# The order and the queue of the first loads of a four-layer kernel

## The chip, the cores and the metric

The kernel runs on one core of a Trainium2 chip. The metric is the device time of one execution in microseconds (us). Every run quoted here is fast, with a granted TensorE clock of 0.999 or 1.000 over the whole run. A profile gives the span of one execution; where a run was profiled, its time as a run is 1.7 to 2.0 us longer than its span. That offset is taken as it is. In lines of the profile PE is TensorE (PEld its weight loads), DVE is VectorE, ACT is ScalarE and SP is SyncE; a q behind the name is the engine's queue of instructions, and L404 is line 404 of the kernel.

## The reference

Four layers on x of 2048 rows by 1024 columns in bf16: layer norm, then linear attention (A), layer norm, then a gated feed-forward (B), and both again with the same weights.

```python
def _layernorm(x, axis=-1, eps=1e-5):
    m = jnp.mean(x, axis=axis, keepdims=True)
    v = jnp.var(x, axis=axis, keepdims=True)
    return (x - m) / jnp.sqrt(v + eps)
...
x = A_x
x = x + _A_ref(_layernorm(x, axis=-1), A_wqkv, A_wo)
x = x + _B_ref(_layernorm(x, axis=-1), B_W_gate, B_W_up, B_W_down)
x = x + _A_ref(_layernorm(x, axis=-1), A_wqkv, A_wo)
x = x + _B_ref(_layernorm(x, axis=-1), B_W_gate, B_W_up, B_W_down)
```

Only the first 20 us matter here: the first four blocks of 128 rows of x are normed, turned over by TensorE and multiplied with the first two column halves (512 columns each) of the key weights, called k0 and k1. q0 is the first half of the query weights.

## The kernel before

The head of the program warms TensorE with ten idle matmuls and issues the first loads, the blocks of x on ScalarE's queue and the weights on SyncE's:

```python
for _ in range(10):
    nc.tensor.matmul(idle, lhsT=zero[:, 0:P], rhs=zero, start=True, stop=True)

k0, k1, v0, q0, q1 = (ring.place() for _ in range(5))
self.load_x(0, 0, nc.scalar)
self.load_x(0, 1)
self.load_x(1, None, nc.scalar)
k0(0, H)
self.load_x(2, None, nc.scalar)
k0(H, 2 * H)
self.load_x(3, None, nc.scalar)
k1()
q0()
self.load_x(4)
...
```

`load_x(t, c)` loads half c of block t, or all of it. `k0(0, H)` loads the first four of k0's eight slices of 128 rows. The sizes are 256 KB for a block of x, 512 KB for half of k0 and 1024 KB for k1 or q0.

What follows is in program order on VectorE and ScalarE, with the work of block 1 woven into that of block 0:

```python
def block0():
    stat(0, 0)
    stat(0, 1)
    rstd(0)
    stat(1, 0)        # block 1's load is waited for here
    scale(0, 0)       # ... ahead of the scale of block 0
    scale(0, 1)
    t0 = turn(0, 0)
    t1 = turn(0, 1)
    t0("s")
    stat(1, 1)
    rstd(1)
    t1("v")
    k(0, 0, between)  # 8 matmuls with k0; turns half of block 1 before the last 2
...
def block1():
    turn(1, 1)("v")
    norm(2)           # block 2's load is waited for here
    k(1, 0)
...
return [block0, block1, lambda: k(0, 1), lambda: block(1, 1, 2), lambda: k(2, 0),
        lambda: block(2, 1, 3), lambda: k(3, 0), lambda: k(3, 1)]
```

## Time and profile before

| | before |
|---|---|
| median of the first 3 runs | 1629.3 us (1629.21 to 1630.51) |
| the profiled run, as a run and as a span | 1630.68 and 1628.9 us |
| TensorE busy | 1621.7 us |
| first projection matmul | 7.46 us |
| fifth projection matmul, after the wait for k0 | 10.23 us |
| VectorE begins the statistics of block 2 | 12.08 us |
| transposes of block 3 | 19.28 us |

TensorE is busy all the time but for the head, so the table is a list of the moments in the head that set the rest. The last row serves as a clock in this document: the span is that moment plus, here, 1628.9 - 19.28 = 1609.6.

### The profile page before, as it was taken

How to read it: one execution, taken by the hardware profiler on the slowest of the kernel's cores; microseconds unless marked ns; L12 is line 12 of the kernel's file. 1: busy time of each engine (PE TensorE's matmuls, PEld its weight loads, DVE VectorE, ACT ScalarE, POOL GpSimd, SP SyncE). 2: the span in 40 equal slices, each digit the busy share in tenths (PEclk: the TensorE clock that was granted, in tenths of full speed). 3: DMA queues.
4: the chain of work that ended last, by engine and by line, in shares of the span. 5: the costliest groups of instructions: out<-in, count | busy, mean ns of one | idle time of the engine just before them, and what ended most of it. 6: DMA issues, size and time to landing. Idle time of an engine off the chain costs nothing.

```text
span 1628.9 us, 18772 instructions
## 1 busy us (share of the span) xinstructions
PE 1621.7 (100%) x7754; PEld 739.3 (45%) x7754; DVE 566.7 (35%) x940; ACT 331.8 (20%) x638; POOL 201.9 (12%) x134
## 2 busy tenths in 40 slices
PE   8999999999999999999999999999999999999999
PEld 4444444444444444444444444444444444444444
DVE  7845695213212222212165547942022111111211
ACT  5741212101110110111066312121011101101110
POOL 2349220000000000000023592100000000000000
DMA  7312647448445444544560147464554454454452
GB/s 245 65 52 56 178 71 206 144 148 232 155 143 190 160 151 161 168 147 137 168 128 1 53 93 250 85 193 146 182 165 152 155 184 155 145 166 154 155 162 71
DMA packets 298246, 235.06 MB, mean 144 GB/s; under 512 B 101296, under 2 KB 294192, under 8 KB 298160
## 3 DMA queue, kind: packets, MB, share of 16 engines
q1 hardware_dynamic: 292832, 228.75, 47.7%
q10 hardware_dynamic: 5328, 5.11, 0.9%
q8 instruction: 60, 0.98, 0.3%
q14 instruction: 26, 0.21, 0.0%
HBM read 201.33 MB, written 8.39 MB: 129 GB/s over the span
## 4 chain that ended last, share of the span: by engine, by line
PE 98%; ACT 1%; DVE 1%; DMA 1%; issue 0%; SPq 0%; DVEq 0%
PE pu L639 24%; PE pg L639 24%; PE acc L663 23%; PE ps L404 12%; PE ps L530 7%; PE ps L439 7%; DMA t<-in_A_wqkv_dram 1%; PE kv L452 0%; PE acc_last L663 0%; ACT e L351 0%; ACT e L350 0%; PE fold L515 0%; DVE st L138 0%; ACT e L352 0%; DVE slab L358 0%
## 5 line engine op out<-in xcount | busy, mean ns | idle before, releaser
L639 PEld LDWEIGHTS <-t 128*128 128x128 bf16 x3584 | 350.3, 98 | 423.2
L639 PE MATMUL pu<-xnT,t 128*128 128x512 bf16 x1792 | 423.5, 379 | 0.0
L639 PE MATMUL pg<-xnT,t 128*128 128x512 bf16 x1792 | 423.4, 379 | 0.0
L663 PE MATMUL acc<-t,hT 128*128 128x512 bf16 x1764 | 382.5, 379 | 0.0
L645 DVE TENSOR_TENSOR hT<-pu,rg 128x512 bf16<-128x512 f32 x224 | 154.7, 691 | 572.0 <-PE pu L639 572.0
L644 ACT ACTIVATE rg<-pg 128x512 f32<-128x512 f32 x224 | 133.5, 596 | 737.3 <-PE pg L639 737.0
L663 PEld LDWEIGHTS <-hT 128*128 128x128 bf16 x1820 | 177.9, 98 | 209.1
L404 PE MATMUL ps<-t,xnT 128*128 128x512 bf16 x1024 | 224.3, 380 | 2.2 <-DMA t<-in_A_wqkv_dram 1.7
L404 PEld LDWEIGHTS <-xnT 128*128 128x128 bf16 x1024 | 99.2, 98 | 122.3 <-issue 4.3
L530 PE MATMUL ps<-T,pqT 128*128 128x512 bf16 x512 | 111.2, 379 | 0.0
L145 ACT ACTIVATE rstd<-mv,eps 128x1 f32<-128x1 f32 x64 | 18.7, 293 | 334.1 <-DVE mv L143 333.9
L680 DVE TENSOR_TENSOR xo<-x,acc 128x512 bf16<-128x512 f32 x31 | 21.3, 688 | 170.3 <-PE acc L663 170.3
L483 POOL TENSOR_TENSOR prod<-pq,zrow 128x1024 f32<-128x1024 bf16 x32 | 67.9, 2122 | 85.9 <-DVE den L488 72.5
L138 DVE BATCH_NORM_STATS2 stats<-x 128x6 f32<-128x512 f32 (+1 forms) x120 | 78.0, 673 | 0.8
L530 PEld LDWEIGHTS <-pqT 128*128 128x128 bf16 x512 | 49.9, 98 | 60.4 <-issue 0.5
L419 POOL CAST ksum<-x 128x512 f32<-128x512 bf16 x2 | 1.7, 866 | 605.4 <-DVE x L358 605.4
L677 DVE TENSOR_TENSOR x<-x,acc 128x512 f32<-128x512 f32 x32 | 21.6, 675 | 138.5 <-PE acc L663 137.4
L421 POOL TENSOR_TENSOR ksum<-ksum,slab 128x512 f32<-128x512 f32 x46 | 54.0, 1183 | 84.6 <-DVE slab L358 75.1
L358 DVE SCALAR_TENSOR_TENSOR pq<-ps,e 128x512 bf16<-128x512 f32 x64 | 44.0, 688 | 53.9 <-ACT e L352 52.2
L495 POOL TENSOR_TENSOR pq<-pq,den 128x1024 bf16<-128x1024 bf16 x32 | 61.7, 1933 | 3.1 <-DVE den L490 3.1
L488 DVE TENSOR_REDUCE den<-prod 128x32 f32<-128x1024 f32 x32 | 39.0, 1217 | 53.9 <-POOL prod L483 53.9
L439 PE MATMUL ps<-slab,x 128*128 128x512 bf16 x256 | 56.6, 379 | 0.0
(57 smaller groups left out, 596.0 us busy)
## 6 DMA issues: line engine op xcount, KB each, us to landing
t<-in_B_W_gate_dram SPq DMA_DIRECT2D x56, 1024.0 KB, 7.1
t<-in_B_W_up_dram SPq DMA_DIRECT2D x56, 1024.0 KB, 5.4
t<-in_B_W_down_dram SPq DMA_DIRECT2D x64, 896.0 KB, 5.2
t<-in_A_wqkv_dram SPq DMA_DIRECT2D x11, 1024.0 KB, 5.6
t<-in_A_wo_dram SPq DMA_DIRECT2D x4, 1024.0 KB, 7.2
away<-x SPq DMA_DIRECT2D x8, 512.0 KB, 4.4
x<-away SPq DMA_DIRECT2D x8, 512.0 KB, 8.5
out_dram<-xo ACTq DMA_DIRECT2D x31, 128.0 KB, 2.5
```

The lines of the kernel that those rows point to most:

```text
L138: self.nc.vector.bn_stats(out=stats[:, c, :], in_=src[:, c * fmax:(c + 1) * fmax])
L358: nc.vector.scalar_tensor_tensor(out=out, in0=ps, scalar=0.0, in1=e, op0=ALU.max, op1=ALU.add)
L404: nc.tensor.matmul(by_row(ps), lhsT=self.xnT[l, l_q][:, kt, j * P:(j + 1) * P], rhs=w[:, kt, :].rearrange("p (b i d) -> p i b d", i=R, d=H ...
L421: nc.gpsimd.tensor_tensor(out=ksum[:, cols], in0=ksum[:, cols], in1=pk, op=ALU.add)
L439: nc.tensor.matmul(ps, lhsT=self.xn[l, t][:, d * P:(d + 1) * P], rhs=self.pk[l, t][:, h * NW:(h + 1) * NW], start=(t == 0), stop=(t == sel ...
L483: nc.gpsimd.tensor_tensor(out=prod, in0=pq_of[sc, j], in1=zrow, op=ALU.mult)
L495: nc.gpsimd.tensor_tensor(out=heads(pq), in0=heads(pq), in1=den[:, :].unsqueeze(2).to_broadcast([P, D // HD, HD]), op=ALU.mult)
L530: nc.tensor.matmul(ps, lhsT=pqT[sc][:, g, j * P:(j + 1) * P], rhs=T[g // 2][:, g % 2, n2 * NW:(n2 + 1) * NW], start=(g == 0), stop=(g == G ...
L639: nc.tensor.matmul(ps, lhsT=w[:, kt, fi * P:(fi + 1) * P], rhs=self.xnT[l, q][:, kt, :], start=(kt == 0), stop=(kt == KT - 1))
L644: nc.scalar.activation(out=rg, in_=pg, func=ACT.Relu)
L645: nc.vector.tensor_tensor(out=h[:, fi, :], in0=pu, in1=rg, op=ALU.mult)
L663: nc.tensor.matmul(ps[:, 0:n], lhsT=hT[ft // 4][:, ft % 4, j * P:(j + 1) * P], rhs=wd[:, k, i * n:(i + 1) * n], start=(ft == 0), stop=(ft ...
```

## The change

The change puts the first loads all on SyncE's queue, in an order meant to bring k0 sooner: block 0, half of k0, block 1, the other half of k0, k1, and only then blocks 2 and 3. The aim is that the second half of k0, for which TensorE waits 1.7 us, no longer shares the way with blocks 2 and 3 (512 KB).

```diff
-        self.load_x(0, 0, nc.scalar)
+        self.load_x(0, 0)
         self.load_x(0, 1)
-        self.load_x(1, None, nc.scalar)
         k0(0, H)
-        self.load_x(2, None, nc.scalar)
+        self.load_x(1)
         k0(H, 2 * H)
-        self.load_x(3, None, nc.scalar)
         k1()
+        self.load_x(2)
+        self.load_x(3)
         q0()
```

## The prediction

> **What bounds the kernel now.** I read the page first, then the waits of TensorE, then the first 30 us as a timeline, as the chain of work and as DMA landings. On the page TensorE is busy 1621.7 of 1628.9 us. The waits view of TensorE over the whole span has four rows, all in the head of the kernel:
> ```profile
> PE ps L404 <- DMA t<-in_A_wqkv_dram: 1.7, 1, 1.7
> PE idle L220 <- DVE zero L217: 1.3, 1, 1.3
> PE tp L260 <- DVE x L154: 0.6, 1, 0.6
> PE ps L404 <- ACT xnT L267: 0.4, 1, 0.4
> ```
> Columns: total us, times, longest. The same view from 20 us on is empty. So all that loads can still give lies before 20 us, and only one row, 1.7 us, names a load: the second half of the first weights (k0). The timeline of the head shows where:
> ```profile
> 0.74 0.40 SPq L369 DMA_DIRECT2D x<-in_A_x_dram  x1
> 0.76 1.97 ACTq L369 DMA_DIRECT2D x<-in_A_x_dram  x4
> 1.19 3.78 SPq L35 DMA_DIRECT2D t<-in_A_wqkv_dram  x4
> 3.78 1.29 DVE L138 BATCH_NORM_STATS2 st<-x 128x6 f32<-128x512 bf16 x2 [2.49 <-DMA x<-in_A_x_dram]
> 5.22 0.68 DVE L138 BATCH_NORM_STATS2 st<-x 128x6 f32<-128x512 bf16 x1
> 5.90 0.74 DVE L154 TENSOR_SCALAR x<-x,mv,rstd 128x512 bf16<-128x512 bf16 x2
> 7.46 1.04 PE L404 MATMUL ps<-t,xnT 128*128 128x512 bf16 x4 [0.37 <-ACT xnT L267]
> 10.23 0.59 PE L404 MATMUL ps<-t,xnT 128*128 128x512 bf16 x2 [1.73 <-DMA t<-in_A_wqkv_dram]
> 12.08 1.28 DVE L138 BATCH_NORM_STATS2 st<-x 128x6 f32<-128x512 bf16 x2
> ```
> Columns: start, length. VectorE takes block 0 at 3.78, the first statistic of block 1 at 5.22, scales block 0 at 5.90; TensorE runs four matmuls of the first projection and stops at 8.50, until k0's second half is there. The last row is the statistics of the third block. The chain of work between 8 and 20 us says what the end depends on after that:
> ```profile
> 1.66 8.53 DMA t<-in_A_wqkv_dram
> 10.19 0.04 issue
> 10.23 0.59 PE ps L404 x2
> ...
> 11.74 0.42 DVE xnT L265
> 12.16 1.20 DVE st L138 x2
> ...
> 18.72 0.51 DVE x L154
> 19.23 0.05 issue
> 19.28 0.62 PE tp L260 x8
> ```
> All but the first lines of it is **VectorE**: from the copy at 11.74 to the scale at 18.72 it works in program order with hardly a gap (busy 0.86 to 1.00 in each microsecond from 12 to 19), and TensorE's 0.6 us wait at 19.28 is for it. From there on the chain never leaves busy engines. So a gain in the head is worth what it moves **VectorE's work at 12.08**, no more.
>
> **What the Trainium skill says.** "DMA: Bandwidth & Descriptors", section "Issuing engines are not separate DMA queues": loads issued from several engines run on the same 16 DMA engines and interleave; several issuers save only issue time. The trace agrees: 388 GB/s at 4 to 5 us with both queues, 350 at 12 to 13 us with SyncE's alone, so one queue loses little bandwidth and the change is one of order. Section "Queues, rings and completion order": each DMA engine takes turns between queues, and completion is not in order of issue. The trace agrees: x block 2, on ScalarE's queue, was issued after half of k0 was, and landed at 7.5, well before it (10.2). Section "Why a DMA increments its semaphore by 16 and not by 1": the 16 engines finish independently and only the full count means landed. In the view of DMA packets in 0.2 us steps the packets under 512 B (with these loads I take them for the completion writes) of k1 come from 10.6 to 13.0 us, so the slowest engine is over 2 us behind the others. That matters below.
>
> **The part removed: ScalarE's four issues and the turn-taking.** They take 1.97 us of ScalarE's queue (row at 0.76); ScalarE's first work on block 0 comes at 5.34, so this frees nothing on the path.
>
> **The part added: the same loads on SyncE.** An issue takes 0.40 to 0.51 us, so the eight first loads go out at about 0.74, 1.19, 1.6, 2.1, 2.6, 3.0, 3.5, 4.0. First bytes move some 1.5 us after an issue (0.74 to 2.2), and each load's turn comes later than that, so issue time is hidden.
>
> **The part moved: the order of bytes.** Landings before, from issue plus time to landing of the DMA view: block 0 at 3.55 and 3.8, block 1 at 5.2, first half of k0 at 5.7, block 2 at 7.5, second half of k0 at 10.2, block 3 at 10.4, k1 at 13.4, q0 at 16.4. I turn this into a landing rate, from 2.2 us on and including the slowest engine: up to the first half of k0, 1024 KB in 3.5 us, 293 KB/us; up to k1, 3072 KB in 11.2 us, 274; up to q0, 4096 KB in 14.2, 288. The second half of k0, 2048 KB in 8.0, had only 256, as part of k1 went beside it. With 274 to 293 KB/us, as an estimate, the new order lands so:
> - block 1: 1024 KB, 5.7 to 5.9 (was 5.2)
> - second half of k0: 1536 KB, 7.4 to 7.8, at 256 KB/us 8.2 (was 10.2)
> - k1: 2560 KB, 10.9 to 11.5 (was 13.4)
> - block 2: 2816 KB, 11.8 to 12.5 (was 7.5)
> - block 3: 3072 KB, 12.7 to 13.4 (was 10.4; used at 14.98)
>
> Now the path. (a) Block 0 comes alone first; its statistic may start up to 0.3 us sooner, and the second half, issued 0.45 us later than before, is needed only 0.6 us after the first. (b) VectorE takes block 1's statistic before it scales block 0, so it waits until about 5.75 instead of 5.22, and block 0's scale goes from 5.90 to 5.75 + 0.68 = 6.43: **0.5 us lost**. (c) The four first matmuls then run from 8.0 to 9.0, and k0's second half is there (8.2 at worst): the wait of 1.73 us is gone, the fifth matmul starts at 9.0 instead of 10.23, **1.2 us gained** on TensorE. (d) VectorE could then take block 2 at 12.08 - 1.2 = 10.9, but block 2 lands at 11.8 to 12.5. Its statistics start between 0.2 us earlier and 0.45 later than now, about **0.1 us later** in the middle. VectorE's chain and with it the end move by that, not by 1.2.
>
> **Rivals.** *The full gain.* If the lag of the slowest engine comes from two queues taking turns, it is gone: 2816 KB at 0.37 MB/us, the rate of the typical engine, is 7.8 us, with 0.5 us to the semaphore it lands at 10.5, before 10.9. Then 1.2 us are gained: 1628.1 us. For it: there is hardly any spread until 5.4 us. Against it: after 10 us SyncE's queue runs alone and the lag stays at 2 us. *A new wait takes its place*, that of block 2, as worked out: 1629.4; at the late end, or if the lag is another half microsecond larger, 1629.8 to 1630.3. *SyncE's queue as the bound*: its fourth weight load took 1.39 us to issue and the next block 4.59 us, so the queue can block when much is outstanding. But block 2 goes out after about as much as stood before that 1.39 us, so its block would be some 1 us, and its turn for the DMA engines comes at about 9.5 us: hidden. *Later loads starve*: q0 and the fifth block keep their place in the sum of bytes (q0 16.4, fifth block 17.05, used near 26.8 and 21.8): hidden.
>
> **Range and chances.** I give the new wait 65% (0.1 us slower) and the full gain or most of it 35% (1.0 us faster): 0.065 - 0.35 = -0.3 us, so 1629.3 - 0.3 = 1629.0 us. The runs before lie between 1629.2 and 1630.5, so scatter is as large as the effect; with the two rivals' ends I take 1627.8 to 1630.6. Two per cent are 32.6 us, ten times all of TensorE's waits: within 2% 0.98, 0.01 on each side.
>
> **What would show it.** TensorE's wait for k0 is gone or under 0.3 us, and its fifth matmul starts near 9.0 (c). VectorE's first statistic of block 1 waits on its load and starts at 5.6 to 6.0 (b). VectorE's statistics of block 2 have a load as releaser and start at 11.8 to 12.5 (d); if they start near 10.9 with no load named, the rival of the full gain holds. The eight transposes of block 3 (19.28 now) move by as much as that start, and the span with them. I am wrong if they move and the span doesn't, if block 2 lands much later than 12.5, or if the order of loads changes what the scheduler makes of the later engine programs, which would show as a difference after 20 us.

## The result, and the profile after

The changed kernel takes 1631.9 us in the median of 4 runs (1631.48 to 1633.01), against 1629.32 for the kernel before in the same session. The ratio is 1.0015, with a 95% interval of 0.9998 to 1.0033. Ratios here are the mean time of one kernel's fast runs over that of the other's fast runs of the same rounds, so they are not quite the ratio of the medians. At the 2% level this is "same", as forecast; but the time lies above the stated range (1627.8 to 1630.6), and all four runs lie above all runs of before. The middle of the forecast, 0.3 us faster, had the other sign, too.

The programs of TensorE, VectorE and GpSimd are instruction for instruction the same in both kernels; only the issues of loads moved. So nothing but landings, and what follows from them, can explain the difference. The waits of TensorE over the whole span of the changed kernel:

```profile
PE tp L260 <- DVE x L154: 2.9, 1, 2.9
PE idle L220 <- DVE zero L217: 1.3, 1, 1.3
PE ps L404 <- ACT xnT L267: 0.3, 1, 0.3
```

The wait of 1.7 us for k0 is gone, as intended. In its place TensorE waits 2.9 us ahead of its first transposes, for VectorE's scale of block 0. The timeline of the head says why (start, length, engine, instruction, and in brackets the idle time before it with what ended it):

```profile
2.13 0.51 SPq L369 DMA_DIRECT2D x<-in_A_x_dram  x1
...
2.98 1.28 DVE L138 BATCH_NORM_STATS2 st<-x 128x6 f32<-128x512 bf16 x2 [1.69 <-DMA x<-in_A_x_dram]
...
7.64 0.69 DVE L138 BATCH_NORM_STATS2 st<-x 128x6 f32<-128x512 bf16 x1 [3.14 <-DMA x<-in_A_x_dram]
8.25 0.72 DVE L154 TENSOR_SCALAR x<-x,mv,rstd 128x512 bf16<-128x512 bf16 x2
...
8.71 1.03 PE L260 MATMUL tp<-ident,x 128*128 128x128 bf16 x8 [2.91 <-DVE x L154]
...
10.00 2.74 PE L404 MATMUL ps<-t,xnT 128*128 128x512 bf16 x6 [0.26 <-ACT xnT L267]
...
14.43 1.27 DVE L138 BATCH_NORM_STATS2 st<-x 128x6 f32<-128x512 bf16 x2
```

The first row is the issue of block 1 at 2.13. Block 0 is used sooner than before, at 2.98 instead of 3.78. Then VectorE waits 3.14 us for block 1, which lands at 7.62 (2.13 plus the 5.49 us that the chain of work gives it); before, its statistic ran at 5.22. Block 0's scale stands behind that statistic in program order and goes from 5.90 to 8.25. The row at 10.00 holds a second surprise: six matmuls take 2.74 us, while before the first four took 1.04. The view of that line of code gives the records of single matmuls in ns (minimum, median, maximum), for the changed kernel from 11 to 12 us:

```profile
L404 PE MATMUL ps<-t,xnT x4: 634/634/634, 10.4 to 11.7; 128*128 128x512 bf16 x4
```

and for the kernel before from 7 to 8 us:

```profile
L404 PE MATMUL ps<-t,xnT x3: 380/380/390, 7.5 to 7.9; 128*128 128x512 bf16 x3
```

TensorE had stood idle from 5.80 to 8.71 and ran at half its pace, a matmul every 0.43 us instead of every 0.22, until about 13.5 us. The Trainium skill describes this on "TensorE: Matmul & The Clock Gate", section "Part 1: The HAM clock gate (the "warmup" mystery)": the array runs at half clock by default, comes up after some 3.4 us of sustained matmuls and goes back when idle. The trace agrees with its figures for 512 columns, 426.7 and 215.7 ns from start to start. The column of the granted clock in the table of windows reads 1.00 in these same microseconds. The records of clock changes that lie behind it are in the packed trace, though no view lists them: the first of this run is the rise to full clock at 13.49 us, and ahead of a first record the column reads 1.00 whatever the clock is. So, as far as the records go, the clock did not fall here: the ten idle matmuls (4.45 us, 0.43 us apart) had not brought it up. In eight of the other profiles it rose between 4.87 and 6.59 us; three traces hold no such record.

The chain of work in the changed kernel:

```profile
2.13 5.49 DMA x<-in_A_x_dram
7.62 0.02 issue
7.64 0.04 DVE st L138
...
10.00 2.74 PE ps L404 x6
12.74 0.43 PE tp L260 x4
...
14.08 0.42 DVE xnT L265
14.51 1.20 DVE st L138 x2
...
21.63 0.62 PE tp L260 x8
```

It runs through block 1's load and the slow matmuls, not through block 2's load, which the forecast had named. The transposes of block 3 come at 21.63 instead of 19.28, and 21.63 - 19.28 = 2.35 is the difference of the spans (1631.2 - 1628.9 = 2.3). For this pair of profiles the sum closes: +2.42 for block 1's statistic (5.22 to 7.64), -1.73 for the wait that is gone, and the rest, 2.35 - 2.42 + 1.73 = 1.66, is nearly all the slow clock (six matmuls at 0.21 us extra are 1.3, the transposes and the last two the rest).

It would be easy to stop here. But a pair of profiles is two executions, and the experiments show that this is only a part of the story.

### The profile page after: what moved, and what is told of

The parts are those of the page before. It is cut to its first block, busy times and chain, and to the rows that moved or that the text cites. A ratio compares the mean times of both kernels' runs of the same rounds, so it can differ in the third digit from the quotient of the medians.

```text
span 1631.2 us, 18772 instructions
## 1 busy us (share of the span) xinstructions
PE 1623.6 (100%) x7754; PEld 740.7 (45%) x7754; DVE 566.5 (35%) x940; ACT 331.6 (20%) x638; POOL 201.9 (12%) x134
## 4 chain that ended last, share of the span: by engine, by line
PE 98%; ACT 1%; DVE 1%; DMA 0%; issue 0%; SPq 0%; DVEq 0%
PE pu L639 24%; PE pg L639 24%; PE acc L663 23%; PE ps L404 12%; PE ps L530 7%; PE ps L439 7%; PE kv L452 0%; PE acc_last L663 0%; DMA x<-in_A_x_dram 0%; ACT e L351 0%; ACT e L350 0%; PE fold L515 0%; DVE st L138 0%; ACT e L352 0%; DVE slab L358 0%
```

## The experiments

The theory at the outset: the changed order costs through block 1, which is late behind half of k0, and through the slow clock that this brings with it. Rivals: block 2 behind k1 sets the pace, as forecast; the single queue itself is slow; the profiles are not typical. Twelve runs were made, of eight new kernels and four repeats, all correct. "Mean against before" is the ratio of fast runs, turned into us with 1629.6.

| run | block 1's statistic, us | block 2's statistics, us (load waited for) | block 3's transposes, us | span, us | median run, us | mean against before |
|---|---|---|---|---|---|---|
| before, first profile | 5.22 | 12.08 (no) | 19.28 | 1628.9 | 1629.3 | |
| before_again_1 | 5.24 | 11.08 (no) | 18.29 | 1627.9 | 1629.42 | 0.9997 |
| before_again_2 | 5.27 | 10.45 (no) | 17.65 | 1627.3 | 1629.04 (one run) | |
| changed, first profile | 7.64 | 14.43 (no) | 21.63 | 1631.2 | 1631.9 | 1.0015, +2.4 us |
| after_again | 6.26 | 12.68 (yes, 0.34) | 19.90 | 1629.5 | 1631.84 | 1.0015, +2.4 us |
| a_after_24_idle | 6.91 | 12.45 (no) | 19.66 | 1629.3 | 1631.49 | 1.0010, +1.6 us |
| i_after_x2_before_k1 | 6.97 | 13.51 (no) | 20.70 | 1630.3 | 1631.44 | 1.0011, +1.8 us |
| d_x1_before_k0 | 5.22 | 12.52 (yes, 1.73) | 19.73 | 1629.3 | 1631.08 | 1.0008, +1.3 us |
| f_before_no_idle | 5.64 | 11.82 (no) | 19.02 | 1628.6 | 1630.55 | 1.0006, +1.0 us |
| c_before_order_one_queue | 5.20 | 10.99 (no) | 18.48 | 1628.1 | 1630.48 | 1.0004, +0.7 us |
| b_x0_x1_on_act | 5.46 | 11.03 (yes, 0.61) | 18.24 | 1627.9 | 1630.11 | 1.0003, +0.5 us |
| h_one_queue_best | 5.94 | 12.21 (no) | 19.41 | 1629.0 | 1629.78 | 1.0002, +0.3 us |
| e_best | 5.32 | 10.20 (no) | 17.39 | 1627.0 | 1628.95 | 0.9999, -0.2 us |
| e_again | 5.25 | 10.12 (no) | 17.32 | 1626.9 | 1628.79 | 0.9994, -1.0 us |

All intervals of the ratios but that of after_again (1.0002 to 1.0027) reach over 1, as the scatter of single runs, up to 2 us, is as large as the effects. So the runs are read together with the profiles, where the mechanism shows.

### Keep TensorE busy in the changed kernel

```diff
-        for _ in range(10):
+        for _ in range(24):
```

> The changed kernel with 24 instead of 10 idle matmuls ahead of the first work, nothing else. In the changed kernel TensorE stands idle from 5.8 to 8.7 us and its first projection matmuls then start every 0.43 us instead of every 0.22. Theory 'cold clock': busy through 5.8 to 8.5, the matmuls from 10.0 us on start every 0.22 us (records of 380 ns, not 634), the copy that VectorE makes at 14.08 comes near 12.8, block 2 (landed at 12.7 in the changed kernel) lets its statistics start near 12.9 instead of 14.43, and the transposes of block 3 come at 20.0 to 20.2 instead of 21.63; span about 1629.7, that is 1.5 us below the changed kernel and still 0.8 above before. Rival 'only the late load of block 1': the matmuls stay slow or the end doesn't move; transposes of block 3 at 21.6, span 1631.2.

Measured: 24 idle matmuls ran from 1.35 to 8.72 us, the first ten at 0.43 us each and the rest at 0.22. The first six projection matmuls took 1.47 us instead of 2.74, so the clock was up (its record rises at 5.47), and the copy on VectorE that had ended the slow stretch at 14.08 came at 12.02. The span was 1629.3, near the 1629.7 expected. The edit is not clean in one respect: the idle matmuls themselves held TensorE until 8.72, while the scale of block 0 was begun at 7.52. From the first transposes to that copy it took 3.46 us instead of 5.37, so by this pair the slow clock cost 1.9 us in the first profile (1.7 by the sum above). The runs gained less than the profile: +1.6 us against before instead of +2.4. A term of the clock is there, but with it gone the kernel is still slow.

### The changed order with block 0 and block 1 back on two queues

```diff
-        self.load_x(0, 0)
+        self.load_x(0, 0, nc.scalar)
         self.load_x(0, 1)
         k0(0, H)
-        self.load_x(1)
+        self.load_x(1, None, nc.scalar)
         k0(H, 2 * H)
```

> The changed order, but the first half of block 0 and block 1 go back to ScalarE's queue; block 2 and 3 stay on SyncE behind k1. Theory 'one queue is late to start and puts block 1 behind half of k0': block 1 lands near 5.2 us again, its statistic starts at 5.2 to 5.4, TensorE stays warm, the second half of k0 lands by 8.2 (it has 512 KB less ahead of it than before) so the wait of 1.73 us is under 0.3; block 2 then limits: lands at 11.8 to 12.7, transposes of block 3 at 19.1 to 19.9, span 1628.7 to 1629.5. Rival 'the order of block 2 and 3 behind k1 alone costs it': block 1 is at 5.2 but the span stays near 1631.

Measured: block 1's statistic came at 5.46, TensorE stayed fast, and no load of k0 was waited for. Block 2 landed at 11.0, somewhat sooner than the 11.8 to 12.7 expected, and VectorE waited 0.61 us for it. The span was 1627.9 and the runs only 0.5 us over before. Most of the loss is gone, but the edit changes the queue as well as block 1's turn, and block 2 landed at 11.01 instead of 12.66 to 12.74, so this run alone doesn't say which of them did it.

### The order of before on one queue

```diff
+        self.load_x(1)
         k0(0, H)
-        self.load_x(1)
-        k0(H, 2 * H)
-        k1()
         self.load_x(2)
+        k0(H, 2 * H)
         self.load_x(3)
+        k1()
         q0()
```

> The order of the kernel before, but all on SyncE's queue: block 0, block 1, half of k0, block 2, half of k0, block 3, k1. Theory 'order': block 1 has only block 0 ahead of it and lands by 5.0 us, TensorE stays warm, the second half of k0 has 2048 KB up to it as before and lands at 9.5 to 10.3, so the end is that of before within 0.5 us: 1628.9 to 1629.4 in the profile. Rival 'the single queue itself' (issue in a row, the DMA engines stand idle between 2.8 and 3.6 us in the changed kernel): the idle of the DMA engines comes again and the span is 1630 or more.

Measured: block 1's statistic at 5.20 and the second half of k0 landed at 9.10, with a wait of 0.76 us for it and a wait of 0.48 us for k1, which landed at 12.81. The span was 1628.1, better than expected of either theory, and the runs 0.7 us over before. **The single queue costs 0.7 us in the mean here, not 2.4.** Two other pairs of runs differ in the queue: block 1 early (1.3 over before on one queue, in the run after this one, and 0.5 on two, in the run before), and the two further orders below (0.3 and -0.2). They read 0.8 and 0.5. Each is within the scatter, but all three have one sign. It does leave a mark. In the table of windows the last figures of a row are the granted clock, the DMA engines' busy share and GB/s. The kernel before from 3 to 4 us:

```profile
3.00:4.00 1.00, 1.00 (x4) 0.42 (x3) 0.22 (x1) 0.00 (x0) 0.00 (x0) 1.00 1.07 385
```

and the changed kernel:

```profile
3.00:4.00 1.00, 1.00 (x4) 0.41 (x3) 1.00 (x2) 0.00 (x0) 0.00 (x0) 1.00 0.69 174
```

With one queue the DMA engines move less than half as much for a microsecond. I read it so, without a run that shows it: the small halves of block 0 are done before the next load, issued 0.92 us after the first, has come to flow. The run with the order of before has the same hole (180 GB/s from 3 to 4 us, 230 from 4 to 5), but there the busy share is 1.13 from 3 to 4, so the engines weren't simply empty. In that run block 1's own packets (2.9 to 4.9 us) fall into the hole, and it still lands at 5.17; in the changed kernel those of half of k0 do, ahead of block 1.

### Block 1 ahead of k0, the rest as changed

```diff
+        self.load_x(1)
         k0(0, H)
-        self.load_x(1)
         k0(H, 2 * H)
```

> The changed kernel with one swap: block 1 ahead of the first half of k0, all on SyncE's queue. Theory 'order of block 1': block 1 lands by 5.0 us (was 7.62), its statistic is no longer waited for beyond that, the first projection matmul comes at 7.5 to 8.0 unless the first half of k0, then fourth in line, lands later than that (6.96 in the changed kernel, with 256 KB more ahead 7.5 to 8.0); TensorE stays warm; block 2 limits at 12.0 to 12.7, transposes of block 3 at 19.3 to 20.0, span 1629.0 to 1629.6. Rival 'the single queue': k0's first half is late too, over 8.5 us, TensorE cools, span over 1630.5.

Measured: as expected, but for block 1, which landed at 5.20 and not by 5.0. The timeline of VectorE:

```profile
5.22 0.69 DVE L138 BATCH_NORM_STATS2 st<-x 128x6 f32<-128x512 bf16 x1 [0.77 <-DMA x<-in_A_x_dram]
...
12.52 1.29 DVE L138 BATCH_NORM_STATS2 st<-x 128x6 f32<-128x512 bf16 x2 [1.73 <-DMA x<-in_A_x_dram]
```

Block 1's statistic is back at 5.22, TensorE is fast, k0 is waited for 0.32 us, and now VectorE waits 1.73 us for block 2, which lands at 12.50. The transposes of block 3 are at 19.73 and the runs 1.3 us over before. This shows the forecast's term by itself: block 2 behind k1 sets a floor of 12.5 us.

### The changed kernel once more

No edit.

> The changed kernel itself once more, on another chip session, to see how much of its profile is chance: is block 1 late again, does TensorE cool again? Theory 'block 1 behind half of k0, then the cold clock': block 1 lands at 6.7 to 7.7 us, the first projection matmuls start every 0.43 us, the transposes of block 3 come at 20.5 to 21.7, mean of the fast runs 2 to 3 us over before. Rival 'one unlucky profile': block 1 lands before 6.2 or the matmuls are fast, and the mean is within 1 us of before.

Measured: the runs repeat, +2.4 us, but the profile doesn't look like the first. The timeline of VectorE and TensorE:

```profile
6.26 0.69 DVE L138 BATCH_NORM_STATS2 st<-x 128x6 f32<-128x512 bf16 x1 [1.71 <-DMA x<-in_A_x_dram]
...
12.68 1.29 DVE L138 BATCH_NORM_STATS2 st<-x 128x6 f32<-128x512 bf16 x2 [0.34 <-DMA x<-in_A_x_dram]
```

```profile
8.62 2.38 PE L404 MATMUL ps<-t,xnT 128*128 128x512 bf16 x6 [0.26 <-ACT xnT L267]
```

Block 1 was used at 6.26 instead of 7.64, below the 6.7 expected. TensorE was still slow for most of its first six matmuls. This time the chain goes through block 2's load, landed at 12.66, and the span is 1629.5. So one and the same kernel ends now by block 1 and the clock, now by block 2. It is the fastest of its five runs that was profiled. Both expectations missed in part: the profile was better than the theory said, and the mean didn't move.

### Two further orders

With block 1 early and block 2 between k0 and k1, first on two queues:

```diff
-        self.load_x(0, 0)
+        self.load_x(0, 0, nc.scalar)
         self.load_x(0, 1)
+        self.load_x(1, None, nc.scalar)
         k0(0, H)
-        self.load_x(1)
         k0(H, 2 * H)
-        k1()
         self.load_x(2)
+        k1()
         self.load_x(3)
         q0()
```

> First half of block 0 and block 1 on ScalarE's queue, the rest on SyncE's in the order second half of block 0, both halves of k0, block 2, k1, block 3, q0. Theory: the head is a chain of three landings (block 1, second half of k0, block 2) and the clock; here block 1 lands by 5.5, k0 by 7.6, block 2 by 9.0, k1 by 11.4, so no load is waited for after block 1. VectorE takes block 2 at 10.3 to 10.5 instead of 12.08, transposes of block 3 at 17.5 to 18.0 instead of 19.28; profile's span 1627.1 to 1627.6, mean of the fast runs 1 to 1.7 us under before, faster than the run with block 2 behind k1 (1627.9 in its profile). Rival 'TensorE or VectorE has another limit there' (k1 in time, 8 matmuls of k1 at 11.7): transposes of block 3 stay at 18.2 or later.

Measured: no load is waited for after block 1, and the chain is TensorE's and VectorE's own work:

```profile
7.47 1.47 PE ps L404 x6
...
10.28 1.20 DVE st L138 x2
...
17.39 0.62 PE tp L260 x8
```

The second half of k0 lands at 7.4 and block 2 at 8.0. The span is 1627.0, a bit better than expected, but the mean is only 0.2 us under before (with one longer run, 1630.5, among five), where 1.0 to 1.7 was expected. That miss pointed at the kernel before: its first profile might not be typical.

The same order with all on SyncE's queue:

```diff
+        self.load_x(1)
         k0(0, H)
-        self.load_x(1)
         k0(H, 2 * H)
-        k1()
         self.load_x(2)
+        k1()
         self.load_x(3)
```

> As the run before it in order, but all on SyncE's queue with block 1 ahead of k0: block 0, block 1, both halves of k0, block 2, k1, block 3, q0. Theory 'order decides, the queue little': block 1 at 5.2, both halves of k0 by 8.8, block 2 by 9.8, k1 by 12.2; a wait for k0 of 0.3 and for k1 of 0.5 at most, transposes of block 3 at 18.0 to 18.6, span 1627.6 to 1628.2, 0.3 to 0.8 above the two-queue form. Rival 'the single queue itself costs the 2 us': span 1630 or more.

Measured: the runs are 0.3 us over before, as expected of order; the profiled run (1630.81) was the slowest of the five and shows how that comes about:

```profile
7.00 1.03 PE L260 MATMUL tp<-ident,x 128*128 128x128 bf16 x8 [1.22 <-DVE x L154]
8.30 2.66 PE L404 MATMUL ps<-t,xnT 128*128 128x512 bf16 x6 [0.26 <-ACT xnT L267]
```

Block 1 landed at 5.92 instead of 5.2. TensorE stood idle for 1.22 us and then ran slow for over 2 us; the first record of its clock is the rise at 10.73, so here, too, the ten idle matmuls had not brought it up. The expected 18.0 to 18.6 became 19.41. Of this delay of some 1.1 us, the slow clock alone accounts for about as much: 2.66 instead of 1.47 us for six matmuls.

### The kernel before without warming

```diff
-        for _ in range(10):
+        for _ in range(1):
```

> The kernel before with one idle matmul instead of ten; loads as before. It measures the cold clock by itself: nothing of the loads moves. Theory 'cold clock': the first projection matmuls start every 0.43 us instead of 0.22 (records of 634 ns instead of 380); 0.21 us more for each of them after the wait for k0 (10.23), some 4 to 12 until the clock is back, so the copy at 11.74 comes 0.9 to 1.5 us later and the transposes of block 3 at 20.2 to 21.0; span 1629.8 to 1631.5. Rival 'the clock is no matter here, as VectorE limits from 12 us on': transposes of block 3 within 0.3 us of 19.28.

Measured, with the loads of before:

```profile
8.00 2.56 PE L404 MATMUL ps<-t,xnT 128*128 128x512 bf16 x6 [0.26 <-ACT xnT L267]
```

The matmuls are slow, and the runs are 1.0 us over before. Block 2 was ready all along, so this is nearly a price of the clock by itself; block 1 was also 0.4 us later in this profile (5.64). The position expected for the transposes (20.2 to 21.0) was too late. It was reckoned from the first profile of before, and in this one the second half of k0 landed at 9.3 and was not waited for.

### The kernel before, profiled twice more

No edit.

> The kernel before, profiled once more. The first profile of it took 1630.7 us as a run, 1.4 over its median, so it may be an unlucky one. Theory 'the second half of k0 landed late by chance in that profile': in a typical run it lands near 9 us, the wait for it is 0.5 us or less instead of 1.7, VectorE takes block 2 at 10.6 to 11.2 instead of 12.08, the transposes of block 3 come at 17.8 to 18.4 and the span is 1627.4 to 1628.0; then the removed wait was mostly not there to win. Rival 'the first profile is typical': wait 1.5 to 1.8 us, span 1628.7 to 1629.1.

> As the run ahead of it, a second look at the kernel before: by the theory the second half of k0 lands between 8.5 and 10.2 us and the span is its start of block 3's transposes plus 1609.6 us; by the rival both looks show the 1.7 us.

Measured: the timeline of TensorE in the first of them and in the second.

```profile
9.23 0.59 PE L404 MATMUL ps<-t,xnT 128*128 128x512 bf16 x2 [0.81 <-DMA t<-in_A_wqkv_dram]
```

```profile
7.42 1.77 PE L404 MATMUL ps<-t,xnT 128*128 128x512 bf16 x6 [0.37 <-ACT xnT L267]
```

The wait for the second half of k0 is 0.81 us in one and doesn't show as a wait in the other: six matmuls run in 1.77 us, against 1.47 with no load late. The load landed at 9.19 and 8.56, against 10.19 in the first profile. VectorE takes block 2 at 11.08 and 10.45. The wait of 0.81 is more than the 0.5 that the theory allowed, but in the main it holds: **the 1.7 us that the change was to save were an unlucky execution.** The spans say the same: of the 25 of before in the three later sessions, with a median of 1627.7, only two reach the 1628.9 of the first profile. As runs these two took 1629.69 and 1629.04, on either side of the median; the first profile took 1630.68.

### Block 2 ahead of k1, block 1 left behind half of k0

```diff
-        k1()
         self.load_x(2)
         self.load_x(3)
+        k1()
         q0()
```

> The changed kernel with blocks 2 and 3 moved ahead of k1, nothing else: one queue, block 1 still behind half of k0. Theory 'two terms: block 2 behind k1 sets the floor at 12.5 to 12.7, block 1 behind half of k0, with the cold clock, is the other': block 2 lands by 10, k1 at 11.7 to 12.7, block 1 still at 6.3 to 7.6, TensorE cold; VectorE takes block 2 at 11.9 to 14.4 as TensorE lets it, the runs lie 0.3 to 1.0 us under the changed kernel and still 1 to 2 over before. Rival 'block 2 is all of it': within 0.5 us of before. Rival 'block 1 is all of it': as the changed kernel, 2.0 to 2.5 over before.

Measured: block 2 landed at 9.1 and was not waited for. Block 1 still landed at 6.95, and then:

```profile
8.04 0.72 PE L260 MATMUL tp<-ident,x 128*128 128x128 bf16 x8 [2.24 <-DVE x L154]
...
9.12 2.74 PE L404 MATMUL ps<-t,xnT 128*128 128x512 bf16 x6 [0.37 <-ACT xnT L267]
```

Here the column of the granted clock does show it, with 0.50:

```profile
10.00:11.00 1.00, 1.00 (x4) 0.40 (x3) 0.48 (x2) 0.00 (x0) 0.00 (x0) 0.50 1.08 376
```

By its records the clock rose at 5.70, fell at 9.11 and rose again at 12.52. So the transposes at 8.04 ran at full pace (0.72 us for eight, against 1.03 in the changed kernel) and the matmuls at 9.12 did not.

The runs are 1.8 us over before and the transposes of block 3 at 20.70. Taking away the late block 2 alone (this run) leaves 1.8 of the 2.4 us; taking away the late block 1 alone (block 1 ahead of k0) leaves 1.3; taking away both on one queue leaves 0.3. So each of the two lateness terms is enough to lose more than a microsecond: one repair alone takes away 0.6 or 1.1 of the 2.4 us, both together 2.1. What lies between 1.3 and 1.8 is within the scatter.

### The better order once more

No edit to the two-queue form.

> The two-queue form with block 2 between k0 and k1 once more, with more rounds, to see whether it is faster than the kernel before as its profile (1627.0) suggests. Theory: block 1 by 5.5, k0 by 7.6, block 2 by 9; span 1627.0 to 1627.3 when the clock is up, 0.3 to 0.9 us under before in the mean of the fast runs. Rival: no difference to before beyond scatter (within 0.3 us), because before's typical run has little wait for k0 either.

Measured: five runs between 1628.64 and 1628.87, mean 1.0 us under before. In the two sessions together nine of the ten runs of this version lie under the fastest run of before in their session (1629.22 and 1629.03). I take it to be better than the kernel before by half a microsecond or so, and than the changed one by some 3, with the note that both intervals of the ratio (0.9985 to 1.0012 and 0.9981 to 1.0006) reach over 1.

## Why the prediction was wrong

By the spans the two kernels are 2.3 us apart: a median of 1630.0 for nine runs of the changed one, 1627.7 for 25 of before. The forecast's start of block 2's statistics, 12.2, means a span of some 1629.0 (12.2, 7.2 more to block 3's transposes as in the first profile, and 1609.6). So, as an estimate, 1.2 us of the miss come from the profile that it started from (1628.9 instead of 1627.7), and 1.0 from what it did not see in the changed kernel: block 1's late landing and the clock. Of its signs, the wait for k0 was gone in the first profile, but the fifth matmul came at 11.68 (forecast 9.0), block 1's statistic at 7.64 (5.6 to 6.0), and block 2's statistics at 14.43 with no load named; in the second profile they came at 12.68 with their load named, close to the forecast.

- **The starting point.** The failed premise is the sentence "TensorE runs four matmuls of the first projection and stops at 8.50, until k0's second half is there", taken for the typical run. In two further profiles that wait was 0.8 us and none to name, and VectorE took block 2 at 11.08 and 10.45, not 12.08. So step (c), "1.2 us gained", had little to gain from, and step (d), which compared the new landing of block 2 with 12.08 and came to "about 0.1 us later", compared it with a figure 1.0 to 1.6 us too late. With 10.45 to 11.08 instead, the same landing of 11.8 to 12.5 would have given some 0.7 to 2.1 us lost. The clue was at hand: the profiled run took 1630.68, 1.4 over the median.
- **Block 2 behind k1, step (d): the mechanism was right.** Its landing was forecast at 11.8 to 12.5 and measured at 12.7 in the first profile, 12.66 in the second and 12.50 with block 1 moved ahead. In the second profile of the changed kernel it ends the chain.
- **Block 1 behind half of k0, steps (a) and (b): right in kind, too small.** Its landing was worked out as 5.7 to 5.9 from landing rates of before, and "0.5 us lost" from it. In four profiles with that order it was used at 6.26, 6.91, 6.97 and 7.64, so 1.0 to 2.4 us were lost. The rate came from a kernel with two queues running. In the changed one the DMA engines moved 174 GB/s from 3 to 4 us instead of 385; the sentence "each load's turn comes later than that, so issue time is hidden" was wrong for the load behind block 0. A hole of that depth is worth, as an estimate, 0.55 us ((385 - 174) / 385 of a microsecond). The packets kept in the traces show where the rest went. The first 1024 KB, block 1 with all ahead of it, had moved by 5.5 to 5.8 us in these four profiles (5.1 in those with two queues), so the rate was about right. But the last of block 1's 128 packets ended at 5.84, 6.44, 6.51 and 7.21, with the landing 0.4 us after it. So what was too small is the allowance for a load's last packets. Why they take so long, and differently in each execution, is not settled.
- **The clock: missing from the sum.** No step asked what TensorE does while VectorE waits for block 1. It stood idle for 1.5 to 2.9 us and then ran its next six matmuls in 2.4 to 2.7 us instead of 1.5. From the first transposes to the copy on VectorE ahead of block 2's statistics, this costs 1.1 to 1.9 us: 4.6 to 5.4 us in these three profiles, and 3.47 in the two-queue form, where no load is late. The run of before without warming puts the price at 1.0 us. This is why repairing block 2 alone still left 1.8 us.
- **The rivals.** "The full gain" had 35% and was refuted by the late block 2 (12.50 to 12.7 us, where the rival said 10.5). "SyncE's queue as the bound" was rightly held to be small: three pairs put one queue at 0.5 to 0.8 us. "Later loads starve" was rightly dismissed, as nothing after 22 us changed.
- **Three readings of the profile before.** The 0.6 us wait of TensorE that the prediction puts at 19.28 is the one at 6.38; ahead of 19.28 TensorE was idle for 0.08 us only. So TensorE was as busy as VectorE from 10.23 on, and VectorE's earlier start alone would not have moved the end; the run with the order of before on one queue ends by TensorE's own chain. Block 2 landed at 9.34, not 7.5 (the 5.8 us added to its issue is the median of two loads, 4.0 and 7.7). And "one queue loses little bandwidth" was read at 12 to 13 us, not in the first microseconds, where it failed. Only this last one bears on the forecast, through block 1. (Two per cent are eight times TensorE's waits of 4.0 us, not ten.)
- **The chances** of 0.98 for "within 2%" were right. The range was too narrow, since it added the scatter of the result but not the scatter of the one profile from which it started.

## What to carry to other kernels

When a head of a few microseconds is to be tuned, compare the time of the profiled run with the median first, and profile the kernel more than once: a wait in one profile is one draw, and here it varied by more than the change was worth. When loads are put in a new order, list every one of them with the moment at which its first use comes in program order; the load brought forward pays with those that it overtakes, and a small one that gates an engine working in program order should go ahead of a large one. And when a landing moves, ask what the matmul engine does in the gap: a gap of one or two microseconds can be paid twice, once as a wait and once as slow matmuls.

## What the Trainium skill lacked or had wrong

- "DMA: Bandwidth & Descriptors", section "Issuing engines are not separate DMA queues", says that several issuers save only issue time, "which is usually small relative to the DMA itself". With the small loads at the start it does not look small: one queue, which needs 0.92 us to get past the two 128 KB halves, moved 166 to 252 GB/s from 3 to 4 us in seven profiles, where two queues moved 359 to 395 in seven others. In the runs this was worth 0.5 to 0.8 us, within their scatter.
- "TensorE: Matmul & The Clock Gate", section "Part 1", has the clock follow a window of 3413 ns that runs free of the kernel. The records of one run agree (changes at 5.70, 9.11 and 12.52 us, block 1 behind half of k0). What the page doesn't say is how little work makes a window idle: in the one that ended with the fall at 9.11 TensorE had worked for some 0.8 us of the 3.41.
- The same section puts the change to the full clock around 4 us into sustained matmuls, 0.5 us more or less from run to run. With 24 idle matmuls in a row the trace agrees: the first ten start 0.43 us apart and the rest, after 4.2 us, 0.22 us apart. But the ten idle matmuls of this kernel (4.45 us) did not bring the clock up in two profiles (first rise at 13.49 and 10.73), and in four the rise came 4.80 to 5.25 us after their start, when they had ended. So such a warming has no margin, and 4.5 us is not enough to count on.
- No page that I read says how much the landing of one load varies between executions of the same program. Here the second half of k0 landed at 10.19, 9.19 and 8.56 us in three profiles of the kernel before.
